# First batch's attention blocks turned with all 128 rows into one bank per head, and the first feed-forward weight converted in two halves

## The chip, the cores and the metric

The kernel runs on one core of a Trainium2 chip. The metric is device time in microseconds (us) of that core. The engines are TensorE (PE in the profile; PEld are its weight loads), VectorE (DVE), ScalarE (ACT), GpSimd (POOL) and SyncE (SP, which here only issues DMAs). Matrix products land in PSUM, which this kernel divides into eight banks; the other engines work in SBUF.

## What is computed

Three stages follow each other: attention with rotary positions (4 batches, 8 heads, 576 positions, 64 wide), a feed-forward block with shifted inputs, and a second one with a spatial gate.

```python
scores = scale * np.matmul(q_rot, k_rot.transpose(0, 1, 3, 2))
attn = np.exp(scores - np.max(scores, axis=-1, keepdims=True))
attn = attn / (np.sum(attn, axis=-1, keepdims=True) + 1e-09)
x = np.matmul(attn, v)                       # then heads side by side: (4, 576, 512)

xk = mu_k * x + (1.0 - mu_k) * x_prev        # x_prev: x one position earlier
xr = mu_r * x + (1.0 - mu_r) * x_prev
k = np.maximum(xk @ w_k, 0.0)                # w_k: 512 x 1024
x = sigmoid(xr @ w_r) * (k * k @ w_v)

h = np.maximum(x @ w_in, 0.0)
u, v = h[..., :512], h[..., 512:]            # v is normalised over its 512 entries
gated = u * (w_spatial @ v + b_spatial)
out = gated @ w_out
```

## The kernel before

**Units.** Attention works on pairs of heads (16 pairs: 4 a batch) and, within a pair, on blocks of 128 queries. 576 is four and a half blocks, so two pairs make nine *units*: eight of 128 queries of both heads of one pair, and a *tail* unit (every m with m % 9 == 4) that holds the 64 left over from each of the two pairs. The first batch is units 0 to 17. For unit m the kernel does this:

- scores (`scores`, L338): eight products with 64 rows each, into `s`, two tiles (one for each head) of two banks each. In the batches after the first, `q` and `k` are split in a high and a low part and L330 makes 12 products instead;
- maxima (`top`, L342, DVE), one for each head;
- exponentials (`expo`, L347, ACT), one for each head, into `pf`. The score products of unit m+1 reuse the banks of `s`, so those of head 0 need the first exponential of unit m and those of head 1 the second;
- sums and their reciprocals: `total` (ACT), `norm` (DVE), `spread` (ACT, writes `rb`);
- turns (`turn`, L367, PE): the 512 *main* keys of `pf` are transposed. Each head takes eight transposes of 64 rows, `turn(0)` and `turn(1)`. Both write a tile `t` of two banks: what comes from query rows 0 to 63 goes to the first bank, that from rows 64 to 127 to the second, so each bank holds a half of both heads. `turn(0)` stands before the scores of unit m+1 in PE's queue, `turn(1)` behind them;
- turn of the rest (`turn_rest`, L380 and L381, PE): the last 64 keys of both heads and `rb`, two transposes of 128 rows, into a tile `u` of one of the two banks of the pool `m`;
- copies out of PSUM into `pt`: `take(1)` and `take(0)` (L395, ACT), and `take_rest` (L402, DVE);
- for every second unit, and for the tail, the product with the values (`values`, L409, ten products over 128 rows, into the other pool `m` bank), and `gather` (L421, DVE) into `xt`.

**Between.** The rotary steps of later pairs (`prep`, L249 and L257) and the conversion of weights run on DVE, ACT and POOL beside the units. The weights arrive as 64-bit floats. Converting one piece of 512 columns (`weight64`) takes three DVE instructions (L156, L164, L165), two on ACT (L160, L171) and two on POOL (L168, L174). `w_k` has eight such pieces: two for each of its four row blocks; `wk_ready` lists them, and each product of the first feed-forward layer (`k_dot`, L505) waits for all eight. `w_v` has eight more.

**Feed-forward.** `feed(b, h)` is the first feed-forward block for half h of batch b. It needs all of batch b's units, so batch b's feed runs beside the units of batch b+1, and nothing of that kind can run beside the first batch.

**What sets the order.** Each action is a step of a `Plan`: an engine, an assumed duration, what it depends on, a rank, and which slot of a resource it takes or gives back (`take`, `give`; L205 gives `t` one slot, that is the tile of two banks as a whole). `order` (L62) plays the steps through and takes for each engine the ready step of lowest rank; the order that comes out is what each engine's queue holds. The waits on the chip are not the plan's: they are set afterwards from which tile an instruction writes and reads.

## Time and profile before

| | |
|---|---|
| time, three runs | 768.33, 773.10, 777.09 us (median 773.1) |
| profiled execution | 773.33 us, of which the span in the profile is 771.5 us |
| granted TensorE clock, mean | 0.989 |
| PE | 723.5 us busy, 94% of the span |
| DVE | 473.5 us, 61% |
| ACT | 456.4 us, 59% |
| POOL | 112.5 us, 15% |
| transposes of 64 rows, L367 | 1152 |
| the copies L395 of them | 144, mean 589 ns |

The times of rows below are us from the start of the span. In the 40 slices of the page, PE is at 3 to 8 tenths in the first six (to 116 us) and at 9 in nearly every later one. The granted clock is a share of full speed: 1.00 stands for 2.4 GHz and 0.50 for 1.2 GHz; a stretch between is a mixture of the two.

### The profile page before, as it was taken

What the parts mean: (1) busy time and instruction counts of PE and PEld (TensorE: products, weight loads), DVE (VectorE), ACT (ScalarE), POOL (GpSimd) and SP (SyncE); (2) the same over time, 40 slices, a digit from 0 to 9 for tenths busy, and PEclk for the clock granted to TensorE, in tenths of its full rate; (3) what the DMA queues carried; (4) which work ended last, traced back from release to release, by engine and by line L of the source; (5) the groups of instructions that cost most, each with busy time, mean ns of one, the idle gap of its engine ahead of it and who ended that gap; (6) DMA issues with size and microseconds to landing.
All of it is one profiled execution on the core that took longest, in us unless ns stands there. A gap on an engine that the chain in (4) does not pass through costs nothing.

```text
span 771.5 us, 15273 instructions
## 1 busy us (share of the span) xinstructions
PE 723.5 (94%) x6208; PEld 636.9 (83%) x6208; DVE 473.5 (61%) x881; ACT 456.4 (59%) x1045; POOL 112.5 (15%) x132
## 2 busy tenths in 40 slices
PE   3787779899999999999999999999999999999998
PEld 2554448698798788888798799989989999998997
DVE  5769898886886986886866444247363342545111
ACT  4667888887877887777887554246334332533211
POOL 2243245012002021022031000002020000101000
PEclk9989899999999999999999999999999999999999
DMA  8355432442543353443351085082201212010101
GB/s 296 117 158 167 132 116 79 149 122 87 177 132 135 119 173 107 134 143 105 119 174 63 16 297 192 25 264 83 62 1 63 63 47 78 17 31 1 62 1 62
DMA packets 35273, 84.20 MB, mean 109 GB/s; under 512 B 4545, under 2 KB 10433, under 8 KB 35202
## 3 DMA queue, kind: packets, MB, share of 16 engines
q1 hardware_dynamic: 34658, 82.63, 32.6%
q8 instruction: 49, 0.80, 0.4%
q10 hardware_dynamic: 544, 0.59, 0.3%
q14 instruction: 22, 0.18, 0.1%
HBM read 60.65 MB, written 22.55 MB: 108 GB/s over the span
## 4 chain that ended last, share of the span: by engine, by line
PE 87%; ACT 5%; DMA 4%; DVE 3%; issue 1%; SPq 1%; ACTq 0%; DVEq 0%
PE v L409 12%; PE mk L505 12%; PE mv L544 11%; PE sp L680 8%; PE r L680 7%; PE u L680 7%; PE hv L744 7%; PE o L680 7%; PE t L367 6%; PE s L330 5%; PE s L338 3%; ACT pt L395 3%; PE u L380 1%; PE s L327 1%; DMA I-6413_6414<-xd 1%; DMA wi<-wd 1%
## 5 line engine op out<-in xcount | busy, mean ns | idle before, releaser
L342 DVE TENSOR_REDUCE sm<-s 128x1 f32<-128x576 f32 x144 | 106.0, 750 | 28.4 <-PE s L330 20.3
L347 ACT ACTIVATE pf<-s,sm 128x576 f32<-128x576 f32 x144 | 106.6, 749 | 10.6 <-DVE sm L342 10.5
L505 PE MATMUL mk<-x,wk 128*128 128x288 f32 x768 | 110.8, 300 | 0.7 <-DVE pt L400 0.7
L544 PE MATMUL mv<-kh,wv 128*128 128x288 f32 x512 | 109.2, 299 | 0.9 <-DVE pt L402 0.5
L505 PEld LDWEIGHTS mk<-x,wk 128*128 128x128 f32 x768 | 104.0, 190 | 1.7 <-PE u L377 0.8
L395 ACT COPY pt<-t 128x512 f32<-128x512 f32 x144 | 77.6, 589 | 41.5 <-PE t L367 40.7
L409 PE MATMUL v<-pt,vt 128*64 128x256 f32 (+1 forms) x640 | 90.8, 433 | 8.5 <-ACT pt L395 8.2
L367 PEld LDWEIGHTS t<-ident,pf 64*128 64x128 f32 x1152 | 56.3, 141 | 47.0 <-ACT pf L347 22.6
L367 PE MATMUL t<-ident,pf 64*128 64x64 f32 x1152 | 68.8, 232 | 21.0 <-ACT pf L347 20.9
L544 PEld LDWEIGHTS mv<-kh,wv 128*128 128x128 f32 x512 | 83.8, 188 | 2.7 <-issue 1.2
L409 PEld LDWEIGHTS v<-pt,vt 128*64 128x64 f32 x640 | 45.7, 144 | 42.9 <-ACT pt L395 11.3
L544 PE MATMUL mv<-kl,wv 128*128 128x288 f32 x256 | 75.7, 296 | 0.4 <-DVE kl L523 0.4
L680 PE MATMUL sp<-ws,vn 128*128 128x288 f32 x384 | 53.9, 295 | 0.0
L680 PE MATMUL r<-xr,wr 128*128 128x288 f32 x384 | 52.5, 296 | 1.2 <-ACT vs L550 1.2
L680 PE MATMUL o<-g,wo 128*128 128x288 f32 x384 | 52.9, 296 | 0.5 <-ACT os L803 0.5
L680 PEld LDWEIGHTS r<-xr,wr 128*128 128x128 f32 x384 | 51.7, 188 | 1.8 <-ACT vs L550 1.5
L680 PEld LDWEIGHTS sp<-ws,vn 128*128 128x128 f32 x384 | 52.4, 188 | 0.7
L680 PEld LDWEIGHTS o<-g,wo 128*128 128x128 f32 x384 | 51.7, 188 | 1.4 <-ACT os L803 1.2
L680 PE MATMUL u<-x,wi 128*128 128x288 f32 x384 | 52.0, 296 | 0.0
L680 PEld LDWEIGHTS u<-x,wi 128*128 128x128 f32 x384 | 51.6, 188 | 0.3
L249 DVE TENSOR_TENSOR raw<-raw,cst 128x1152 f32<-128x1152 f32 (+1 forms) x34 | 46.7, 1380 | 5.8 <-DMA raw<-kp 5.3
L544 PEld LDWEIGHTS mv<-kl,wv 128*128 128x128 f32 x256 | 48.2, 188 | 0.6 <-DVE kl L523 0.6
(346 smaller groups left out, 1182.0 us busy)
## 6 DMA issues: line engine op xcount, KB each, us to landing
raw<-kp SPq DMA_DIRECT2D x15, 576.0 KB, 3.9
raw<-qp SPq DMA_DIRECT2D x15, 576.0 KB, 4.7
vt<-vp SPq DMA_DIRECT2D x16, 320.0 KB, 3.8
xd<-xt SPq DMA_DIRECT2D x16, 288.5 KB, 4.3
vd<-vs SPq DMA_DIRECT2D x32, 144.0 KB, 1.8
v<-vd SPq DMA_DIRECT2D x16, 288.0 KB, 2.8
out<-os SPq DMA_DIRECT2D x15, 288.0 KB, 2.1
wi<-wd SPq DMA_DIRECT2D x8, 512.0 KB, 9.1
```

What stands on the lines that cost most here:

```text
L249: nc.vector.tensor_tensor(t["raw", k][:, :, z], t["raw", k][:, :, z], cst[:, :, z], op=ALU.mult)
L330: nc.tensor.matmul(ps[j][:, h, :HALF], t[a, 0][r, 128 * c:128 * c + 128], t[b, 1][r, x], **f)
L338: nc.tensor.matmul(o, q[r, 128 * c:min(128 * c + 128, S)], k[r, h * HALF:(h + 1) * HALF], start=True, stop=True)
L342: nc.vector.tensor_reduce(st["sm"][:, 0, j:j + 1], st["s"][j][:, :, :HALF], axis=AX.XY, op=ALU.max, negate=True)
L347: nc.scalar.activation(st["p"][:, j, :].rearrange("p (a b) -> p a b", a=2), st["s"][j][:, :, :HALF], AF.Exp, bias=st["sm"][:, 0, j:j + 1], ...
L367: nc.tensor.transpose(st["t"][:, h, 4 * n + c, :], st["p"][r, n, k:k + 128], ident[r, r])
L395: nc.scalar.copy(o, st["t"][:, :, 4 * k:4 * k + 4, :])
L409: nc.tensor.matmul(pv[HEAD[j], z], v[:, 4 * j + c if c < 4 else 8 + j, :], pt[:, 4 * j + c if c < 4 else 8, z], start=c == 0, stop=c == 4)
L505: nc.tensor.matmul(ps[:, :HALF], wk[w][:, c, fc * 128:(fc + 1) * 128], a[:, c, :], start=k == 0, stop=k == 11)
L544: nc.tensor.matmul(xs["v", dc][:, :HALF], wv[w][:, fc, dc * 128:(dc + 1) * 128], a, start=k == 0, stop=k == 23)
L680: nc.tensor.matmul(ps[:, h, :HALF], w, a[:, h * HALF:(h + 1) * HALF], start=m == 0, stop=m == n - 1)
L744: nc.tensor.matmul(ps[:, :FS], x[a][:, d, c:c + 128], wi[w][:, d, FS:], start=k == 0, stop=k == 11)
```

## The change

Two edits, and a third that follows from them.

1. *Turns of the first batch.* One tile `both` of the two banks is made once. In units 0 to 17 each head's main keys are turned by four transposes of 128 rows (`turn_whole`) into one bank; the rest goes into a bank of `both` too, and no longer into one of `m`. The plan sees two slots, `t`, and gives one to each of the three turns of a unit; each copy gives its slot back. Head 0 and head 1 are copied by `take_whole` (ACT, 512 columns from one bank), the rest by `take_rest` as before. In tail units the transposes keep 64 rows (eight a head); their copies become four of 256 columns.
2. *`w_k` in two parts.* The pieces 0, 2, 4, 6 (columns 0 to 511) stand first, with the old ranks; the pieces 1, 3, 5, 7 get ranks 16.5 to 19.5, among `w_v`'s ranks of 17 to 21.9. Products for the first four column blocks wait for the first four pieces alone, the others for the second four.
3. Units from 18 on turn as before; the plan now calls their tile's slot `d`, and it waits for all copies of the first batch.

```diff
@@ -124,6 +124,8 @@
     v_dram = [dram.tile([128, 4, S], F32, tag=f"vd{b}", name=f"vd{b}") for b in range(B)]
 
     cst = at.tile([128, 2, S], F32, name="cst")
+    both_banks = ps_t.tile([128, 2, 8, 64], F32, tag="t", name="both")
+    whole = []
     ends = [[at.tile([128, 128], F32R, tag=f"qe{i}{k}", name=f"qe{i}{k}") for k in range(2)] for i in range(2)]
     ident = const.tile([128, 128], F32, name="ident")
     mix4 = const.tile([128, NP, 4], F32, name="mix4")
@@ -202,7 +204,7 @@
     wv = [wpool.tile([128, NFC, DM], F32R, tag=f"wB{i}", name=f"wv{i}") for i in range(2)]
 
     second, fed = {}, set()
-    plan = Plan({"m": 2, "e": 4, "t": 1, "ww": WB, "wg": GB})
+    plan = Plan({"m": 2, "e": 4, "t": 2, "d": 1, "ww": WB, "wg": GB})
     add = plan.add
 
     def which(m):
@@ -368,8 +370,8 @@
 
         def turn_rest(slot):
 
-            pt, p = ps_m.tile([128, 4, 128], F32, tag=f"m{slot}", name=f"u{m}"), st["p"]
-            st["u"] = pt
+            p = st["p"]
+            pt = st["u"] = ps_m.tile([128, 4, 128], F32, tag=f"m{slot}", name=f"u{m}") if isinstance(slot, int) else slot
             if tail:
                 for u in range(2):
                     for k in range(2):
@@ -379,6 +381,31 @@
             else:
                 nc.tensor.transpose(pt[:, 0, :], p.rearrange("p a b -> p (a b)")[:, 512:640], ident)
                 nc.tensor.transpose(pt[:, 1, :], st["r"].rearrange("p a b -> p (a b)"), ident)
+
+        def turn_whole(n, slot):
+
+            pt = st["t", n] = both_banks[:, slot].rearrange("p a b -> p (a b)").rearrange("p (c q) -> p c q", c=4)
+            p = st["p"]
+            if tail and n < 2:
+                for u in range(2):
+                    for c in range(4):
+                        k = 64 * n + 128 * c
+                        nc.tensor.transpose(pt.rearrange("p c (h q) -> p (c h) q", h=2)[:, 4 * u + c, :],
+                                            p[HEAD[n], u, k:k + 128], ident[HEAD[n], HEAD[n]])
+            elif n < 2:
+                for c in range(4):
+                    k = 64 * n + 128 * c
+                    nc.tensor.transpose(pt[:, c, :], p[:, n, k:k + 128], ident)
+            else:
+                turn_rest(pt)
+
+        def take_whole(n):
+            x = st["t", n].rearrange("p c (h q) -> p (c h) q", h=2)
+            for u in range(len(into)):
+                if tail:
+                    nc.scalar.copy(turned_to(u)[:, 4 * n:4 * n + 4, 256:320], x[:, 4 * u:4 * u + 4, :])
+                else:
+                    nc.scalar.copy(turned_to(u)[:, 4 * n:4 * n + 4, 128 * part:128 * part + 128], st["t", n])
 
         def turned_to(u):
             d = into[u if tail else 0]
@@ -436,14 +463,28 @@
         nm = add("DVE", 0.17, norm, [t], m - 0.3)
         sp = add("ACT", 0.26, spread, [nm], m - 0.3)
         late = [y for d in into for y in freed.get(d["n"] - PTB, [])]
-        t = add("PE", 0.27, lambda slot: turn(0), [exps[m, 0]], m + -0.02, take="t", kind="s")
-        turned[m, 0] = x = add("PE", 0.27, lambda: turn(1), [exps[m, 1], t], m + 0.05, kind="s")
-        x = add("ACT", 0.59, lambda: take(1), [x] + late, m - 0.2, 0.05)
-        x = add("ACT", 0.59, lambda: take(0), [x] + late, m - 0.2, give=t)
-        turned[m, 1] = t = add("PE", 0.55 if tail else 0.22, turn_rest, [sp], m + 0.2, take="m", kind="t")
-        y = add("DVE", 0.55 if tail else 0.42, take_rest, [t] + late, m - 0.2, give=t)
-        for d in into:
-            d["ev"] += [x, y]
+        if w[0][0] < EXACT:
+            ready = [[exps[m, 0], exps[m, 1]] if tail else [exps[m, 0]], [exps[m, 1]], [sp]]
+            xs = []
+            for n in range(3):
+                turned[m, n] = t = add("PE", (0.5, 0.5, 0.8)[n] if tail else (0.44, 0.44, 0.22)[n], lambda slot, n=n: turn_whole(n, slot),
+                                       ready[n], m + 0.1 * n, take="t", kind="t")
+                if n < 2:
+                    xs.append(add("ACT", 0.68 if tail else 0.59, lambda n=n: take_whole(n), [t] + late, m - 0.2, give=t))
+                else:
+                    xs.append(add("DVE", 0.55 if tail else 0.42, take_rest, [t] + late, m - 0.2, give=t))
+            whole.extend(xs)
+            for d in into:
+                d["ev"] += xs
+        else:
+            t = add("PE", 0.27, lambda slot: turn(0), [exps[m, 0]] + whole, m + -0.02, take="d", kind="s")
+            turned[m, 0] = x = add("PE", 0.27, lambda: turn(1), [exps[m, 1], t], m + 0.05, kind="s")
+            x = add("ACT", 0.59, lambda: take(1), [x] + late, m - 0.2, 0.05)
+            x = add("ACT", 0.59, lambda: take(0), [x] + late, m - 0.2, give=t)
+            turned[m, 1] = t = add("PE", 0.55 if tail else 0.22, turn_rest, [sp], m + 0.2, take="m", kind="t")
+            y = add("DVE", 0.55 if tail else 0.42, take_rest, [t] + late, m - 0.2, give=t)
+            for d in into:
+                d["ev"] += [x, y]
         if part and k != 3 or tail:
             v = add("PE", 2.9 if duo["cols"] > 256 else 2.3, values, duo["ev"] + [vloads[w[0][0]]], m + 0.9, take="m", kind="v")
             i = w[0][0]
@@ -523,7 +564,7 @@
                 nc.vector.tensor_tensor(kl, xs["r", q], raw(kh), op=ALU.subtract)
 
             q = fc // 2
-            z = p = add("PE", 1.58, lambda slot, k_dot=k_dot: k_dot(0, slot), done + wk_ready + [second.get("close")], rank(fc), take=room)
+            z = p = add("PE", 1.58, lambda slot, k_dot=k_dot: k_dot(0, slot), done + wk_ready[fc // 4] + [second.get("close")], rank(fc), take=room)
             free = kept.get(("kl", 8 * b + 4 * h + q - RLB))
             r = add("ACT", 0.42, relu, [p, free], rank(fc) - 2, give=z)
             last.append(p)
@@ -567,7 +608,7 @@
         if i < ROT // 2:
             prep(i)
     mix_ready = add("DVE", 0.4, mixes, [add("SP", 1.0, load_mixes, [], 0, 12)], 6)
-    wk_ready, wv_ready = [], []
+    wk_ready, wv_ready = ([], []), []
 
     def weight_steps(t, r, old=()):
         w = a = add("SP", 0.4, lambda slot: t[0](slot), old, r - 8 if not old else r, 8 if not old else 5, take="ww")
@@ -579,10 +620,11 @@
         a = add("POOL", 1.4, lambda: t[6](), [a], r, give=g)
         return a if len(t) == 7 else add("SP", 0.4, lambda: t[7](), [a], r, 3.5, give=w)
 
-    for c in range(16):
+    for c in (0, 2, 4, 6, 1, 3, 5, 7, *range(8, 16)):
         k = c < 8
         args = (w_k, c // 2, wk[0][:, c // 2], wk[1][:, c // 2], c % 2) if k else (w_v, c - 8, wv[0][:, c - 8], wv[1][:, c - 8], 0)
-        (wk_ready if k else wv_ready).append(weight_steps(weight64(*args), 1.8 * c if k else 17 + 0.7 * (c - 8)))
+        (wk_ready[c % 2] if k else wv_ready).append(
+            weight_steps(weight64(*args), 17 + 0.7 * (c - 8) if not k else 16 + c / 2 if c % 2 else 1.8 * c))
     early = ([(w_r, c, 0, w_dram[0][:, c]) for c in range(NP)]
              + [(w_in, c, q, w_dram[1 + q][:, c]) for q in (1, 0) for c in range(NP)]
              + [(w_out, c, 0, w_dram[3][:, c]) for c in range(NP)])
```

How the queues change, in three places. `pf7` and `pf8` are the exponentials of units 7 and 8, `rb7` the spread reciprocals, `s16` to `s19` the scores of units 8 and 9; in brackets stand the engines whose semaphore the instruction waits for.

PE, from the scores of unit 8 to the first turn of unit 8. Before:

```order
L338 MATMUL s16_600<-rot1_1_276,rot1_0_279 128x288
L338 MATMUL s17_601<-rot1_1_276,rot1_0_279 128x288
L367 MATMUL t7_588<-ident_95,pf7_562 128x64 x8
L380 MATMUL u7_621<-ident_95,pf7_562 128x128 [waits PE_49]
L381 MATMUL u7_621<-ident_95,rb7_585 128x128 [waits Activation_49]
L367 MATMUL t8_634<-ident_95,pf8_630 128x64 [waits PE_49,Activation_49]
L367 MATMUL t8_634<-ident_95,pf8_630 128x64 x7
```

And of the change:

```order
L340 MATMUL s16_525<-rot1_1_254,rot1_0_257 128x288
L340 MATMUL s17_526<-rot1_1_254,rot1_0_257 128x288
L398 MATMUL both_91<-ident_96,pf7_507 128x128 [waits Activation_49]
L398 MATMUL both_91<-ident_96,pf7_507 128x128 x3
L382 MATMUL both_91<-ident_96,pf7_507 128x128
L383 MATMUL both_91<-ident_96,rb7_533 128x128
L398 MATMUL both_91<-ident_96,pf8_551 128x128 [waits DVE_49,Activation_49]
L398 MATMUL both_91<-ident_96,pf8_551 128x128 x3
```

The sequence is the same; the turns are four of 128 rows. New are two waits: the turn of head 1 of unit 7 waits for ACT (the value it waits for is the one that head 0's copy reaches), and the first turn of unit 8 waits for DVE (the copy of unit 7's rest).

ACT, in the same unit. Before:

```order
L358 COPY rb7_585<-sm7_534 128x128 [waits DVE_49]
L160 ACTIVATE I-459_460<-I-459_460 128x512 [waits DMAHW4_49]
L171 CAST wk0_99<-I-575_576 128x512 [waits Pool_49]
L395 COPY pt3_624<-t7_588 128x2x4x64 [waits PE_49]
L395 COPY pt3_624<-t7_588 128x2x4x64
L347 ACTIVATE pf8_630,sm8_602<-s16_600,sm8_602 128x576 [waits DVE_49]
```

And of the change:

```order
L360 COPY rb7_533<-sm7_475 128x128 [waits DVE_49]
L408 COPY pt3_535<-both_91 128x4x128 [waits PE_49]
L173 CAST wk0_100<-I-509_510 128x512 [waits Pool_49]
L408 COPY pt3_535<-both_91 128x4x128 [waits PE_49]
L349 ACTIVATE pf8_551,sm8_527<-s16_525,sm8_527 128x576 [waits DVE_49]
```

One of the two copies has moved ahead. The second one still stands in front of the next unit's exponential, and the value of PE's semaphore that it waits for is reached only by L383, the last transpose of the unit's rest.

DVE, in the same unit. Before:

```order
L354 RECIPROCAL sm7_534<-sm7_534 128x2 [waits Activation_49]
L421 TENSOR_TENSOR xt1_597<-v6_564,pt2_424 128x320 [waits PE_49]
L342 TENSOR_REDUCE sm8_602<-s16_600 128x1 [waits PE_49]
L402 COPY pt3_624<-u7_621 128x2x128 [waits PE_49]
L342 TENSOR_REDUCE sm8_602<-s17_601 128x1
```

And of the change:

```order
L448 TENSOR_TENSOR xt1_521<-v6_495,pt2_376 128x320 [waits PE_49]
L356 RECIPROCAL sm7_475<-sm7_475 128x2 [waits Activation_49]
L344 TENSOR_REDUCE sm8_527<-s16_525 128x1 [waits PE_49]
L429 COPY pt3_535<-both_91 128x2x128 [waits Activation_49]
L344 TENSOR_REDUCE sm8_527<-s17_526 128x1
```

The copy of the rest stands between the two maxima of the next unit in both. Before it waits for PE; in the change it waits for ACT, for the second of the copies above. It stands like this in 13 of the units 1 to 17, in front of both maxima in units 7 and 10, behind both in the other two.

## Rows read from the trace of the kernel before

**Rows 1.** The page's chain of work that ended last, shares of the span by engine.
```profile
PE 87%; ACT 5%; DMA 4%; DVE 3%; issue 1%; SPq 1%; ACTq 0%; DVEq 0%
```

**Rows 2.** Busy time by stretch: start:end, length, engines (instructions), granted clock, DMA share, GB/s.
```profile
36.00:46.00 10.00, 9.22 (x70) 5.58 (x72) 7.00 (x13) 6.56 (x18) 5.51 (x3) 0.66 0.46 148
...
46.00:84.00 38.00, 26.90 (x276) 17.54 (x275) 32.98 (x61) 30.52 (x74) 12.14 (x11) 1.00 0.46 139
...
84.00:93.00 9.00, 8.88 (x70) 5.06 (x66) 7.92 (x17) 6.51 (x18) 3.18 (x2) 0.62 0.53 186
...
120.00:220.00 100.00, 96.74 (x996) 82.56 (x994) 81.41 (x155) 80.90 (x204) 18.68 (x16) 1.00 0.34 113
220.00:600.00 380.00, 373.37 (x3305) 335.93 (x3302) 237.78 (x447) 239.97 (x557) 44.68 (x55) 1.00 0.37 122
```

**Rows 3.** Timeline, units 8 to 9: start, length, engine, line, operation, count, idle before.
```profile
55.63 1.19 PE L338 MATMUL s<-rot,rot 64*128 64x288 f32 x8
...
56.66 0.41 PE L367 MATMUL t<-ident,pf 64*128 64x64 f32 x8
56.86 0.76 DVE L342 TENSOR_REDUCE sm<-s 128x1 f32<-128x576 f32 x1 [0.91 <-PE s L338]
...
57.00 0.33 PE L380 MATMUL u<-ident,pf 128*128 128x128 f32 x1
...
57.11 1.07 ACT L395 COPY pt<-t 128x512 f32<-128x512 f32 x2 [0.52 <-PE t L367]
...
57.16 0.27 PE L381 MATMUL u<-ident,rb 128*128 128x128 f32 x1
57.53 0.41 DVE L402 COPY pt<-u 128x256 f32<-128x256 f32 x1
57.86 0.75 DVE L342 TENSOR_REDUCE sm<-s 128x1 f32<-128x576 f32 x1
58.07 0.76 ACT L347 ACTIVATE pf<-s,sm 128x576 f32<-128x576 f32 x1
58.79 0.75 ACT L347 ACTIVATE pf<-s,sm 128x576 f32<-128x576 f32 x1
...
60.52 0.40 PE L338 MATMUL s<-rot,rot 64*128 64x288 f32 x1
```

**Rows 4.** Timeline, the scores of units 10, 11 and 12, and a value product between.
```profile
65.18 1.19 PE L338 MATMUL s<-rot,rot 64*128 64x288 f32 x8
...
70.58 0.40 PE L338 MATMUL s<-rot,rot 64*128 64x288 f32 x1
...
72.39 2.38 PE L409 MATMUL v<-pt,vt 128*64 128x256 f32 x20 [0.80 <-ACT pt L395]
...
74.70 0.47 PE L367 MATMUL t<-ident,pf 64*128 64x64 f32 x8
...
75.00 1.19 PE L338 MATMUL s<-rot,rot 64*128 64x288 f32 x8
```

**Rows 5.** Timeline, DVE's three instructions that convert one piece of a weight.
```profile
65.34 0.42 DVE L156 TENSOR_SCALAR I-718_719<-I-459_460 128x512 f32<-128x512 f32 x1
...
65.79 0.43 DVE L164 TENSOR_SCALAR I-459_460<-I-459_460 128x512 int32<-128x512 int32 x1
...
66.25 0.69 DVE L165 SCALAR_TENSOR_TENSOR I-718_719<-I-718_719,I-459_460 128x512 int32<-128x512 int32 x1
```

**Rows 6.** Timeline, three value products of 320 columns, and the first two feed-forward products.
```profile
40.97 4.59 PE L409 MATMUL v<-pt,vt 128*64 128x320 f32 x20
...
52.49 2.91 PE L409 MATMUL v<-pt,vt 128*64 128x320 f32 x20 [0.74 <-ACT pt L395]
...
87.50 5.21 PE L409 MATMUL v<-pt,vt 128*64 128x320 f32 x20
...
115.98 3.18 PE L505 MATMUL mk<-x,wk 128*128 128x288 f32 x12
...
120.70 1.83 PE L505 MATMUL mk<-x,wk 128*128 128x288 f32 x12
```

## The prediction

> **What bounds the kernel now.** I read the page's chain of the work that ended last first: PE holds 87% of the span in it, and no other engine more than 5% [rows 1]. Then the busy time by stretch. From 120 us on PE is full: 96.74 us of 100, then 373.37 of 380 [rows 2]. Work there comes in PE's own order, so what delays the start of the second batch delays the end one for one. Between 46 and 84 us, in the first batch, PE is busy for 26.90 us of 38 and DVE for 32.98 [rows 2]: nothing is full, and a chain of waits sets the pace. So the question is how long that chain becomes in units 0 to 17.
>
> Its links stand in the timeline. I call T the end of a unit's scores. For unit 8, T = 55.63 + 1.19 = 56.82, and the next scores end at 60.52 + 0.40 = 60.92: 4.10 us later. In between: the second turn ends at 57.07, the rest's at 57.43; the two copies hold ACT until 58.18 (57.11 + 1.07); DVE takes the first maxima, the copy of the rest (57.53 to 57.94), the second maxima (to 58.61); the exponentials start at 58.07 and 58.79, and the second ends at 59.54; the scores of head 1, which need it, end 1.38 later [rows 3]. Where a value product stands between, the distance is longer: unit 11's scores end at 70.98 and unit 12's at 76.19, 5.21 apart, with the product of 2.38 us beginning at T + 1.41 and ending just before the turn at 74.70 [rows 4].
>
> **The turns and their waits.** The tile `both` is one tile, and the waits that are set for it treat it as one. The three order places show the result: the turn of head 1 waits for the copy of head 0; the copy of head 1 waits for the last transpose of the rest, although it reads the other bank; the copy of the rest waits on ACT for the copy of head 1; and the next unit's first turn waits for the copy of the rest. What was three loose copies is now one line, and the copy of the rest stands in front of the second maxima. I follow it from T, in a transition without a value product.
>
> - Turns. Eight transposes of 64 columns take 0.41, so about 0.05 each; with 128 columns I take 0.10 each, an estimate from that row; the last counts with the 0.33 of a single one [rows 3]. Four: 0.33 + 3 x 0.10 = 0.63. The rest's first transpose begins 0.07 before the turn of before ended (57.00 against 57.07), so PE is free for head 1 at T - 0.07; its turn ends at T + 0.56, and the two of the rest 0.20 later, at T + 0.76. Head 0's copy, which head 1's turn waits for, is done by then: it needs only the first exponential, a scores' length earlier.
> - Head 1's copy starts 0.04 behind its releaser, as 57.11 does behind 57.07: T + 0.80. It takes 0.59 (the table's mean) and ends at T + 1.39. In before both were over at T + 1.36.
> - Copy of the rest: 0.10 behind (57.43 to 57.53), then 0.41: T + 1.49 to T + 1.90. In before T + 0.71 to T + 1.12.
> - Second maxima: begin 0.08 before that copy's end, as in 57.86 against 57.94: T + 1.82, and with 0.75 end at T + 2.57. In before T + 1.79.
> - Exponentials: the first stands behind head 1's copy on ACT, and starts at about T + 1.3 (before T + 1.25), so it ends near T + 2.1 and isn't the limit. The second starts 0.10 behind the maxima, T + 2.67, and ends at T + 3.42 (before T + 2.72).
> - Scores end 1.38 later: T + 4.80 against T + 4.10. That is **+0.70**.
>
> The next unit's first turn waits for the copy of the rest (T + 1.90) as well as for the exponential (T + 2.1): nothing. Behind head 1's copy on ACT wait only the first exponential, as said, and conversion work, which isn't on the path.
>
> There are 18 transitions, from unit 0 to unit 18. Nine are like this: 9 x 0.70 = 6.3. In unit 10 the copy of the rest stands in front of both maxima (unit 7, where it does too, has a value product before it): it ends at T + 1.90, the maxima end at T + 2.57 and 3.23, the second exponential runs from T + 3.33 to 4.08, and the scores end at T + 5.46. The same place was at 70.98 - 66.37 = 4.61 in before [rows 4]: +0.85. Seven have a value product. It waits for head 1's copy, T + 1.44 instead of T + 1.41, +0.03; the copy of the rest only feeds its last products, later. Behind it the turn takes 0.63, and the scores can start 0.56 behind its start instead of 0.30 (74.70 to 75.00): +0.26. 7 x 0.29 = 2.0. In the two tail units the first turn now waits for both exponentials and stands in front of the scores. If it binds, the scores end 0.56 + 1.19 = 1.75 behind the second exponential instead of 1.38; if the value product of that place covers it, nothing. I take 0.2 each, half, 0.4 in all (bounds 0 and 0.74). The first transition, before the pattern has settled, I give 0.3 (bounds 0 and 0.7). Sum: 6.3 + 0.85 + 2.0 + 0.4 + 0.3 = 9.85, about **10 us**.
>
> Weighed against a rule: the rows of before show two engines at work in different banks at once, ACT copying from `t` from 57.11 on while PE turns the rest into `u` at 57.16 [rows 3]. The Trainium skill, PSUM — Partial Sum Buffer, section "PSUM bank collisions raise a hardware error", says that two engines on different banks run clean, and that the dependency is one of bank, not of more. By that rule no wait between the two banks is needed and the sum would be the 776 of the rival "banks apart" below, by the waits that are set 783; no run of before shows a wait of this tile.
>
> **The weight.** The program order has 12 conversions of pieces in front of the maxima of unit 18 before, and 11 after: one piece leaves the first batch. Per piece DVE spends 0.42 + 0.43 + 0.69 = 1.54 us [rows 5]. Its load, one DMA on SP's queue, moves with it; the DMA engines are at 0.46 to 0.53 in the first batch [rows 2] and have room. At most 1.5 us is gained, if all of it stood on the path; but DVE's idle time is where it lies (32.98 of 38 busy, and the chain above leaves DVE free from the second maxima to the next first ones). I take 0. The conversions pushed behind unit 18 meet a DVE at 81.41 of 100 and an ACT at 80.90, with PE full [rows 2]: hidden, 0. There remains the feed-forward's first product: it now needs four pieces only, but stands behind the second turn of unit 19 in PE's queue, later by one unit's scores. In the rows it ran at 115.98 for 3.18 us, the next one at 120.70 for 1.83 [rows 6]. If the move lets it run at the higher clock, 1.35 is gained; if PE stands idle in its stead, up to 1.83 is lost. I take 0.
>
> The profiled execution took 773.33 us, practically the median of 773.1. 773.33 + 9.85 = 783.2: forecast **783 us**. Its own range: 783.2 - 1.35 - 1.5 - 0.7 (no cost in tails and first) = 779.6, and with the dearer ends 783.2 + 1.83 + 0.34 + 0.4 = 785.8; the 0.10 of a transpose could be 0.16 (the pitch from 57.00 to 57.16 [rows 3]), which adds 5 x 0.06 = 0.3 in ten transitions, 3 us: up to 788.8. So 779 to 789.
>
> **The rivals.**
>
> *A clock that falls more often.* The granted clock is 0.66 in 36 to 46 us and 0.62 in 84 to 93, at 1.00 in 46 to 84 [rows 2]; both low stretches are those of the tail units, where value products are far apart and PE only turns and scores. A value product of 320 columns costs 4.59 and 5.21 us there against 2.91 at full clock: 1.68 and 2.30 more [rows 6]. Longer waits stretch every gap between value products. If two to five more places fall, at about 2.0 each, 4 to 10 us come on top: 787 to 793, say 788. Against it: the stretches between are not at the edge in any row, 46 to 84 is at 1.00 throughout. The Trainium skill, TensorE: Matmul & The Clock Gate, section "Part 4: PE-mode transpose", says that transposes do not count as PE-busy for the clock in the same way as products do. That would let the clock fall in gaps that only turns fill, as here, and the trace agrees so far as its low stretches are such (0.66, 0.62).
>
> *A clock that stays up.* Full-row turns keep PE's rows busier; if this saves both low stretches and the first feed-forward product, 1.68 + 2.30 + 1.35 = 5.3 are gained from the sum: 778. Against it: the transposes' columns are the same in total per head, and the waits grow.
>
> *Banks apart.* If the waits between the banks are met before they bind (the rest's transposes being early, or the copies shorter), the copy of the rest stays where it was and only the longer turn is left: 0.11 in each of the ten without a value product, 0.29 in seven, 1.1 + 2.0, with nothing in the tails: 776. Against it: the rest stands behind head 1's turn in PE's queue, so its copy can't be early.
>
> *Not slower.* One of the two copies leaves ACT's place in front of the exponential. If DVE placed the copy of the rest behind both maxima on the chip's path, the first exponential would start at about T + 0.85 and the second right behind it, some 0.35 earlier than now in ten transitions: -3.5; with 2.0 for the value transitions and -1.5 for the piece of weight, 773.3 - 3.0 = 770. It decides if the copy of the rest ends before T + 1.04, the end of the first maxima less the lag. The order of DVE, where it stands between the maxima, speaks against it.
>
> **How the numbers follow.** My forecast gets 0.55, the falling clock 0.18, the clock that stays up 0.12, banks apart 0.08, not slower 0.07. The range 774 to 792 leaves out the last and the far end of the second, less than 2 in 10. One per cent, about what a measurement of this kernel can tell from no change, is 765.4 to 780.8. Slower by over 1%: nearly all of the forecast's 0.55 less its low end (0.10), and the falling clock's 0.18, 0.63, less something for costs that overlap otherwise than drawn: 0.58. Within 1%: the low end, 0.12, 0.08 and most of 0.07: 0.37. Faster: 0.05, where the clock that stays up and the mechanism of the last rival meet.
>
> **What would show it.** In the timeline of the changed kernel: a copy of the rest that begins 1.5 us after T instead of 0.7, its idle time ended by ACT; second maxima at T + 1.8; scores 4.8 apart without a value product; `both` released by ACT at head 1's turn with no idle time. The second batch should begin about 10 us later, and the time behind it stay the same. I am wrong if the scores stay 4.1 apart, if the first batch's clock differs, or if PE's time behind 120 us changes by more than 2 us.

## The result and the profile after

The changed kernel takes **783.76 us** (median of 4 runs, 780.26 to 785.18); the kernel before, beside it, 771.89 (4 runs, 768.33 to 777.09). The ratio is 1.0136, with a 95% interval of 1.0097 to 1.0176: slower, by about 12 us. The forecast was 783, the range 774 to 792. The profiled execution has a span of 781.6 us against 771.5 and a mean granted clock of 0.987 against 0.989.

The chain of work that ended last, shares of the span by engine:

```profile
PE 85%; ACT 5%; DVE 4%; DMA 3%; issue 1%; SPq 0%; POOL 0%; ACTq 0%; DVEq 0%
```

PE still sets the end, with a little less than the 87% of [rows 1], and DVE has one share more. The changed transition stands in the timeline from unit 8 to unit 9, the same place as [rows 3]; the columns are as there.

```profile
58.33 1.24 PE L340 MATMUL s<-rot,rot 64*128 64x288 f32 x8
...
59.50 0.66 PE L398 MATMUL both<-ident,pf 128*128 128x128 f32 x4
59.60 0.76 DVE L344 TENSOR_REDUCE sm<-s 128x1 f32<-128x576 f32 x1 [1.15 <-PE s L340]
...
60.10 0.27 PE L383 MATMUL both<-ident,rb 128*128 128x128 f32 x1
60.41 0.59 ACT L408 COPY pt<-both 128x512 f32<-128x512 f32 x1 [0.35 <-PE both L383]
60.89 0.75 ACT L349 ACTIVATE pf<-s,sm 128x576 f32<-128x576 f32 x1
61.03 0.42 DVE L429 COPY pt<-both 128x256 f32<-128x256 f32 x1 [0.67 <-ACT pt L408]
61.37 0.75 DVE L344 TENSOR_REDUCE sm<-s 128x1 f32<-128x576 f32 x1
...
62.15 0.74 ACT L349 ACTIVATE pf<-s,sm 128x576 f32<-128x576 f32 x1 [0.42 <-DVE sm L344]
62.37 1.90 PE L340 MATMUL s<-rot,rot 64*128 64x288 f32 x8
```

T is 58.33 + 1.24 = 59.57. The new line of waits can be read from the brackets: head 1's copy (60.41) was released by L383, the last transpose of the rest; DVE's copy of the rest (61.03) by that copy on ACT, after 0.67 us in which DVE stood idle; the second maxima follow it (61.37), and the second exponential them (62.15). The scores end at 62.37 + 1.90 = 64.27, 4.70 after T, where [rows 3] had 4.10.

In unit 10 the copy of the rest stands in front of both maxima. T is 69.88 there:

```profile
70.72 0.59 ACT L408 COPY pt<-both 128x512 f32<-128x512 f32 x1 [0.58 <-PE both L383]
...
71.34 0.42 DVE L429 COPY pt<-both 128x256 f32<-128x256 f32 x1 [0.63 <-ACT pt L408]
...
71.68 1.41 DVE L344 TENSOR_REDUCE sm<-s 128x1 f32<-128x576 f32 x2
...
73.20 0.73 ACT L349 ACTIVATE pf<-s,sm 128x576 f32<-128x576 f32 x1
...
73.94 1.37 PE L340 MATMUL s<-rot,rot 64*128 64x288 f32 x8
```

They end at 75.31, T + 5.43; in [rows 4] it was 4.61.

How far the kernel after lies behind the one before, by the end of a unit's scores (us):

| unit | before | after | behind |
|---|---|---|---|
| 4 | 34.03 | 34.53 | 0.50 |
| 9 | 60.92 | 64.27 | 3.35 |
| 12 | 76.19 | 80.91 | 4.72 |
| 14 | 85.91 | 92.06 | 6.15 |
| 15 | 94.14 | 98.77 | 4.63 |
| 18 (first of the second batch) | 107.93 | 115.97 | 8.04 |
| 21 | 126.07 | 134.18 | 8.11 |
| end of span | 771.5 | 781.6 | 10.1 |

8 us are lost in the first batch and 2 more later. Between units 14 and 15 something is won back. That is the clock, by the same stretches as [rows 2]:

```profile
36.00:46.00 10.00, 8.46 (x66) 5.87 (x66) 7.47 (x16) 6.39 (x18) 2.65 (x3) 0.83 0.49 172
46.00:84.00 38.00, 30.66 (x189) 19.22 (x190) 29.08 (x53) 27.04 (x64) 9.74 (x10) 0.96 0.33 108
84.00:93.00 9.00, 6.55 (x46) 4.63 (x42) 5.88 (x13) 6.91 (x20) 3.80 (x3) 0.81 0.57 175
```

The granted clock is 0.83 and 0.81 in the two stretches of the tail units, where it was 0.66 and 0.62, and 0.96 in the one between, where it was 1.00. The value products of 320 columns show both sides:

```profile
41.98 3.45 PE L436 MATMUL v<-pt,vt 128*64 128x320 f32 x20
...
53.92 3.89 PE L436 MATMUL v<-pt,vt 128*64 128x320 f32 x20
...
94.11 2.91 PE L436 MATMUL v<-pt,vt 128*64 128x320 f32 x20
```

The two at the tails took 4.59 and 5.21 before [rows 6] and take 3.45 and 2.91 now; the one at 53.92 took 2.91 and takes 3.89.

The start differs too, and the granted clock doesn't tell it: it is given as 1.00 for the first 30 us of the kernel before. A value product of 256 columns takes 4.53 us there, against 2.38 in [rows 4]. The changed kernel's turn of one head takes 0.66 us at 18.54 already, as at 59.50. The first line is the kernel before, the second the changed kernel:

```profile
22.86 4.53 PE L409 MATMUL v<-pt,vt 128*64 128x256 f32 x20 [0.55 <-ACT pt L395]
```

```profile
18.54 0.66 PE L398 MATMUL both<-ident,pf 128*128 128x128 f32 x4 [1.41 <-ACT pf L349]
```

So the changed kernel leaves its slow start earlier in these two profiles: from unit 1 to 2 it takes 5.37 us, the kernel before 5.84.

### The profile page after: what moved, and what is told of

Read it like the earlier page. It is cut to its first block, busy times and chain, and to the rows that moved or that the text cites. A ratio compares the mean times of both kernels' runs of the same rounds, so it can differ in the third digit from the quotient of the medians.

```text
span 781.6 us, 15025 instructions
## 1 busy us (share of the span) xinstructions
PE 734.1 (94%) x6080; PEld 641.8 (82%) x6080; DVE 475.3 (61%) x881; ACT 459.1 (59%) x1049; POOL 109.4 (14%) x132
## 4 chain that ended last, share of the span: by engine, by line
PE 85%; ACT 5%; DVE 4%; DMA 3%; issue 1%; SPq 0%; POOL 0%; ACTq 0%; DVEq 0%
PE mv L585 11%; PE mk L546 11%; PE v L436 10%; PE sp L722 8%; PE r L722 7%; PE u L722 7%; PE hv L786 6%; PE o L722 6%; PE s L332 5%; PE t L369 4%; PE s L340 3%; PE both L398 2%; PE s L329 1%; PE u L382 1%; ACT pf L349 1%
## 5 line engine op out<-in xcount | busy, mean ns | idle before, releaser
L422 ACT COPY pt<-t 128x512 f32<-128x512 f32 x108 | 58.5, 589 | 29.7 <-PE t L369 29.3
L369 PEld LDWEIGHTS t<-ident,pf 64*128 64x128 f32 x864 | 39.1, 138 | 18.7 <-issue 6.9
L369 PE MATMUL t<-ident,pf 64*128 64x64 f32 x864 | 48.1, 229 | 2.6 <-ACT pf L349 2.6
```

The source lines that it names most:

```text
L369: nc.tensor.transpose(st["t"][:, h, 4 * n + c, :], st["p"][r, n, k:k + 128], ident[r, r])
L422: nc.scalar.copy(o, st["t"][:, :, 4 * k:4 * k + 4, :])
```

## Reading runs at one clock

The runs of one and the same kernel differ by their mean granted clock. Beside the experiments the kernel before was run 63 times: at 0.993 its runs average 769.7 us (14 runs), at 0.984 773.0 (19), at 0.980 775.4 (8). A straight line through the 63 falls by 0.435 us for each 0.001. In the table below the last column moves each run to 0.993 by that slope and takes the mean. It is a fit, good to about 1 us: what a lower clock costs depends on what runs in the stretch, and the mean leaves out the slow start.

| kernel | median us (runs) | ratio, 95% interval | median clock | at clock 0.993 |
|---|---|---|---|---|
| before | 772.7 (63) | | 0.984 | 769.9 |
| after | 783.76 (4) | 1.0136 [1.0097, 1.0176] | 0.986 | 780.1 |
| turns only | 783.99 (4) | 1.0127 [1.0066, 1.0188] | 0.984 | 779.9 |
| weight only | 766.36 (10) | 0.9924 [0.9892, 0.9955] | 0.993 | 766.3 |
| after, two tiles | 771.07 (10) | 0.9980 [0.9953, 1.0007] | 0.991 | 770.3 |
| after, rest in `m` | 771.61 (10) | 0.9989 [0.9962, 1.0017] | 0.991 | 771.0 |
| after, rest copied late | 778.66 (10) | 1.0074 [1.0044, 1.0103] | 0.989 | 776.8 |
| after, first product put back | 782.55 (4) | 1.0136 [1.0091, 1.0181] | 0.983 | 778.0 |
| weight only, six products unread | 777.31 (10) | 1.0057 [1.0028, 1.0085] | 0.998 | 779.4 |
| after, six products unread | 792.80 (4) | 1.0269 [1.0220, 1.0318] | 0.989 | 791.1 |
| weight only, two products unread | 768.23 (10) | 0.9934 [0.9914, 0.9954] | 0.994 | 768.5 |
| weight only, later pieces held | 785.66 (4) | 1.0171 [1.0115, 1.0228] | 0.985 | 782.3 |
| before, rest copied late | 772.24 (10) | 0.9987 [0.9966, 1.0008] | 0.994 | 772.3 |

At one clock the change costs 780.1 - 769.9 = 10.2 us.

## The experiments

The theory: the tile `both`, waited for as one, puts three copies in one line, and that line costs most of the loss. The rivals: the longer turns, the clock, or the weight edit.

### Turns only

```diff
-    wk_ready, wv_ready = ([], []), []
+    wk_ready, wv_ready = [], []
...
-    for c in (0, 2, 4, 6, 1, 3, 5, 7, *range(8, 16)):
+    for c in range(16):
```

> The changed kernel with the old order of the weight pieces (all eight pieces of w_k at their old ranks, every product of the first feed-forward layer waits for all eight). In the program the first feed-forward product then stands again ahead of unit 20's scores. Theory (the line of waits in the first batch costs about 8 us, and 1.9 us of the 10 come from the first feed-forward product that moved behind unit 20's scores): the first batch stays as long as in the changed kernel, and the end comes 1.9 us earlier than there, near 782 us, a ratio of 1.010 to 1.013 to the kernel before. Rival (the weight edit itself is what costs, by conversions pushed into the second batch): most of the loss goes, 773 to 777, ratio under 1.007.

783.99 us, ratio 1.0127. The rival falls: without the weight edit the loss is all there (779.9 at one clock, after 780.1). The 1.9 us that the theory wanted back don't show there. In the profiles the time from the end of unit 18's scores to the end is 664.47 us, 1.2 less than in the changed kernel (665.63, below). The stretch from 146.15 to 166.15 us has a granted clock of 0.91, with PE busy for 16.82 us of 20: something was given back there, in a program whose second batch is laid out differently. This run doesn't settle the size of that term.

### Weight only

The kernel before, with the opposite of that edit.

> The kernel before with the weight edit alone: two parts of w_k, the turns as before. The first feed-forward product keeps its old place in PE's queue. Theory (one piece less in the first batch is worth nothing, and the later pieces are hidden): the time of before within 1.5 us, ratio 0.998 to 1.002. Rival 1 (the piece stood on the path): 1.5 us gained or more, ratio 0.998 or lower. Rival 2 (conversions in the second batch delay it): 775 to 780, ratio 1.004 to 1.010.

766.36 us, ratio 0.9924: rival 1, in sign, but four times its size, 6.2 us. The stretches of [rows 2] and [rows 6] show where most of it is:

```profile
36.00:46.00 10.00, 8.05 (x92) 5.24 (x94) 7.99 (x18) 8.28 (x21) 5.04 (x4) 1.00 0.74 241
...
84.00:93.00 9.00, 6.67 (x70) 4.28 (x68) 8.31 (x15) 8.19 (x21) 3.08 (x2) 1.00 0.57 187
```

The clock stays at 1.00 in both stretches of the tail units. Both value products of 320 columns there take 2.91 us, the transitions that hold them 5.81 and 5.74 instead of 8.16 and 8.23. Of the 6.8 us that unit 18's scores come earlier, 4.8 are in these two transitions. (At one clock the whole gain is 3.6.) Two transitions at full clock are 0.5 shorter each (from unit 3 to 4: 4.69 instead of 5.21; from unit 10 to 11: 4.10 instead of 4.61). In the second of these the copy of the rest now stands between the maxima instead of in front. Behind unit 21's scores the kernel needs 645.34 us, before 645.43: what was put into the second batch is hidden there. Why the clock holds at the tails with this order of work no run shows; the last experiment shows it holding at one of them without this edit.

### Two tiles

```diff
-    both_banks = ps_t.tile([128, 2, 8, 64], F32, tag="t", name="both")
+    pw = ps_w.enter_context(tc.tile_pool(name="ps_w", bufs=1, space=PSUM, side="right"))
+    banks2 = [pw.tile([128, 8, 64], F32, tag=f"w{i}", name=f"both{i}") for i in range(2)]
...
-            pt = st["t", n] = both_banks[:, slot]...
+            pt = st["t", n] = banks2[slot]...
```

(The pool is closed before unit 18's turn, which takes its two banks as one tile again.)

> The changed kernel with the two banks as two tiles, in the same order of instructions on every engine; only the waits differ: head 1's copy waits for its own four transposes, the copy of the rest for the rest's two. Theory (the waits across the banks are the price): in a transition without a value product head 1's copy starts at T + 0.63 instead of T + 0.84, the copy of the rest at T + 0.90 instead of T + 1.46, the second maxima at T + 1.24 instead of T + 1.80, and the scores end 4.2 apart instead of 4.7; ten of these give 4.8 us, those with a value product up to 1.4: 777 to 780 us, ratio 1.006 to 1.009, the rest being the moved feed-forward product and longer turns. Rival (the longer turns and the clock are the price, not the waits): within 1.5 us of the changed kernel, ratio 1.012 to 1.015.

771.07 us, ratio 0.998: 12.7 us less than the changed kernel, of which 9.8 at one clock. That is well below the 777 to 780 of the theory, which had 6.2 us of gain. The order of instructions is the same on every engine. The same transition, from unit 8, with T = 51.17:

```profile
51.10 0.66 PE L402 MATMUL both<-ident,pf 128*128 128x128 f32 x4
...
51.71 0.27 PE L387 MATMUL both<-ident,rb 128*128 128x128 f32 x1
51.80 0.59 ACT L412 COPY pt<-both 128x512 f32<-128x512 f32 x1 [0.31 <-PE both L402]
52.08 0.42 DVE L433 COPY pt<-both 128x256 f32<-128x256 f32 x1
52.28 0.75 ACT L350 ACTIVATE pf<-s,sm 128x576 f32<-128x576 f32 x1
52.43 0.75 DVE L345 TENSOR_REDUCE sm<-s 128x1 f32<-128x576 f32 x1
...
53.21 0.74 ACT L350 ACTIVATE pf<-s,sm 128x576 f32<-128x576 f32 x1
53.76 1.57 PE L341 MATMUL s<-rot,rot 64*128 64x288 f32 x8
```

Head 1's copy begins at T + 0.63, released by its own turn (L402); the copy of the rest at T + 0.91, beside it; the second maxima at T + 1.26; the scores end at T + 4.16. The numbers expected were 0.63, 0.90, 1.24 and 4.2.

So the line is as long as the theory says, and yet more comes back than it counts. Unit 18's scores end at 102.67, 13.3 us earlier than in the changed kernel. Six transitions run at full clock in both profiles. Together they give 2.0 us: 0.54 (unit 8 to 9), 0.55 (17 to 18), and about 0.2 each in the two with a value product of 256 columns (9 to 10, 11 to 12) and the two that lead into a tail unit. Nearly all the rest lies in transitions in which one of the two kernels has a low clock. How much of the 9.8 is the line itself, and how much the clock that went with it, no run separates.

In these rows ACT (51.80 to 52.39) and DVE (52.08 to 52.50) copy from the two banks at once. This is the rule weighed in the prediction: the Trainium skill, PSUM — Partial Sum Buffer, section "PSUM bank collisions raise a hardware error", asks for a dependency within one bank only. The rows agree with it.

### The rest in `m` again

```diff
-                                       ready[n], m + 0.1 * n, take="t", kind="t")
+                                       ready[n], m + 0.1 * n, take="t" if n < 2 else "m", kind="t")
...
+            if n == 2:
+                return turn_rest(slot)
```

> The changed kernel with the turn of the rest written to a bank of the pool m again, as before the change; the main keys keep their four transposes of 128 rows and their bank per head, and the two banks stay one tile. The order of instructions is that of the changed kernel; head 1's copy waits for its own turn, the copy of the rest for the rest's transposes. Theory (the whole price of the waits comes from the rest having joined the tile): as with two tiles, 769 to 773 us, ratio 0.996 to 1.001. Rival (the two heads' banks hinder one another as well, so that only separate tiles help): 775 to 781, ratio 1.004 to 1.011.

771.61 us, in the theory's range, as with two tiles (771.0 against 770.3 at one clock). The tile of two banks may stay one tile: what cost the time is that the rest was turned into it.

### The rest copied late

```diff
-                    xs.append(add("DVE", ..., take_rest, [t] + late, m - 0.2, give=t))
+                    xs.append(add("DVE", ..., take_rest, [t] + late, m + 0.45, give=t))
```

> The changed kernel with one number altered: the copy of the rest ranks behind both maxima of the next unit on DVE (it stands there in all units now). All waits stay. Theory (it is the second maxima behind that copy that is late): second maxima at T + 0.8 to T + 1.55, the first exponential stays at T + 1.3, the second follows it at T + 2.05, scores 4.1 to 4.2 apart: 5 us back, 777 to 780, ratio 1.006 to 1.010. Rival (head 1's copy, late on ACT in front of the first exponential, is enough to cost it; or the next unit's first turn then waits for the later copy): no gain, ratio 1.012 to 1.015.

778.66 us, ratio 1.0074, in the theory's range; 3.3 us less at one clock, where 5 were expected. The transition from unit 8, T = 60.17:

```profile
60.55 1.41 DVE L344 TENSOR_REDUCE sm<-s 128x1 f32<-128x576 f32 x2
...
61.02 0.59 ACT L408 COPY pt<-both 128x512 f32<-128x512 f32 x1 [2.02 <-PE both L383]
61.50 0.75 ACT L349 ACTIVATE pf<-s,sm 128x576 f32<-128x576 f32 x1
61.88 0.41 DVE L429 COPY pt<-both 128x256 f32<-128x256 f32 x1
...
62.23 0.74 ACT L349 ACTIVATE pf<-s,sm 128x576 f32<-128x576 f32 x1
```

Head 1's copy is as late as in the changed kernel (T + 0.85), and still the scores end at T + 4.18, because both maxima are done before the copy of the rest. Four other transitions without a value product take 4.16 or 4.17. So in these it is the place in front of the second maxima that the loss goes through, as the theory has it; ACT's late copy alone costs 0.1. What became of the rest of the 5 us is shown in one place only: with the copy of the rest planned later, PE has unit 8's value product behind unit 9's first turn (it starts 2.8 us after T, not 0.7), and unit 10's scores end 6.34 after unit 9's, where it was 5.61. From unit 11 to 12, with a value product too, it is 5.61 in both. The profile's clock is lower as well (0.982 against 0.987).

### The first feed-forward product put back

```diff
+    first_k = []
...
-        scored[m] = s = add("PE", ..., need + [exps.get((m - 1, j)) for j in range(2)], m - 1.0, kind="s")
+        scored[m] = s = add("PE", ..., need + [exps.get((m - 1, j)) for j in range(2)] + ([first_k[0]] if m == 20 else []), m - 1.0, kind="s")
...
+            first_k.append(p)
```

> The changed kernel with one dependence more in the plan: unit 20's scores come behind the first feed-forward product, as in the kernel before; unit 19's second turn and rest come ahead of them too. Theory (the product that moved leaves twelve products more to do behind unit 21's scores, 1.9 us): the stretch from the end of unit 21's scores to the end is 645.4 us as in the kernel before, not 647.4; 781 to 783 us, ratio 1.010 to 1.014. Rival (TensorE only waits elsewhere for it): the same as the changed kernel, 783 to 785, ratio 1.013 to 1.017.

782.55 us: too near the changed kernel to tell by the medians alone; at one clock 778.0 against 780.1, 2.1 less. The trace tells it better. The stretch from the end of unit 21's scores to the end, in the kernel before, the changed kernel, and this one:

```profile
126.07:771.50 645.43, 631.43 (x5400) 575.42 (x5396) 372.72 (x695) 367.18 (x827) 67.52 (x86) 1.00 0.30 99
```

```profile
134.18:781.60 647.42, 634.48 (x5412) 577.72 (x5408) 375.87 (x699) 370.09 (x833) 71.47 (x88) 1.00 0.30 98
```

```profile
133.74:778.30 644.56, 631.78 (x5400) 575.28 (x5396) 374.22 (x698) 368.86 (x829) 68.50 (x87) 1.00 0.29 99
```

The changed kernel has 5412 products left at that point, the other two 5400: the twelve of one column block, 1.83 us in [rows 6]. They make 647.42 - 645.43 = 2.0 us in this stretch, and they go away with the dependence. But the stretch begins behind the place where the product moved, so what was done there instead isn't counted. From the end of unit 18's scores, ahead of that place, the same three kernels need:

```profile
107.93:771.50 663.57, 646.96 (x5553) 587.70 (x5548) 388.22 (x727) 382.71 (x866) 77.16 (x93) 1.00 0.30 100
```

```profile
115.97:781.60 665.63, 648.91 (x5551) 588.76 (x5550) 390.44 (x729) 383.31 (x867) 79.17 (x95) 1.00 0.31 101
```

```profile
113.95:778.30 664.35, 647.72 (x5551) 587.60 (x5550) 390.15 (x729) 383.62 (x867) 78.32 (x95) 1.00 0.30 101
```

The changed kernel needs 2.06 us more than the kernel before, and 1.28 of them go away with the product put back; in the kernel with the turns only it was 1.16. Where the other 0.8 lies no run shows.

### Later pieces held

The kernel with the weight edit alone, the pieces made in two further groups, each waiting for a unit's scores:

```diff
+        if m == 13:
+            pieces((1, 3, 5, 7), [scored[m]])
+        if m == 16:
+            pieces(range(8, 16), [scored[m]])
```

> The kernel before with the weight edit alone, and the second four pieces of w_k held until the scores of unit 13, those of w_v until the scores of unit 16: 7 conversions instead of 11 (and 12 in the kernel before) stand in front of the maxima of unit 18. Theory (a conversion costs the first batch only where it stands between two maxima or shifts the copy of the rest, not by its time): the first batch as long as with the weight edit alone, 764 to 768, ratio 0.989 to 0.995, unless the later products of the feed-forward have to wait. Rival (each piece costs the first batch 1.5 us and more): four pieces less give 4 to 6 us more, 760 to 762, ratio under 0.987.

785.66 us, far above both ranges. The first batch is no shorter with four conversions less: unit 18's scores end at 103.29 (weight only 101.16, with the low clock elsewhere). From the end of unit 7's scores to there both kernels run at full clock, this one first:

```profile
49.20:103.29 54.09, 40.02 (x416) 25.91 (x414) 39.67 (x80) 42.12 (x106) 6.32 (x5) 1.00 0.36 116
```

```profile
47.77:101.17 53.40, 40.57 (x415) 26.21 (x414) 46.36 (x94) 45.00 (x112) 17.13 (x16) 1.00 0.39 128
```

With 6.7 us less work on DVE the stretch is 0.7 us longer. So the time of the conversions taken out cost the first batch nothing, as I had put it. The second batch pays for the delay:

```profile
120.00:220.00 100.00, 87.87 (x824) 72.66 (x822) 86.93 (x150) 74.02 (x182) 30.91 (x23) 0.93 0.38 125
```

PE is busy for 87.87 us of 100 there, in [rows 2] for 96.74.

### Products that nobody reads

```diff
+            def filler(slot):
+                f = ps_m.tile([128, 512], F32, tag=f"m{slot}", name=f"f{m}")
+                for _ in range(6):
+                    nc.tensor.matmul(f[:, :HALF], qk[w[0][0]][0][:, 0:128], qk[w[0][0]][1][:, 0:HALF], start=True, stop=True)
```

> The kernel before with the weight edit alone, and in the first batch, behind the rest's transposes of each unit that no value product follows, six products of 128x128 by 288 columns into a free bank of m that nobody reads (they compute nothing that is used). TensorE waits there for about 1.3 us; the six take about 0.9. Theory (the clock falls where TensorE has had little to do, and each 0.001 of mean granted clock is worth about 0.5 us by the spread of the runs of one kernel): the stretches at 1.2 GHz in the first batch disappear, mean clock from 0.993 to 0.997 or more, 762 to 765 us, ratio 0.987 to 0.991. Rival (the clock does not follow that, or the products delay the next turn by as much): 766 to 770, ratio 0.992 to 0.997.

> The changed kernel with the same six unread products behind the rest's transposes of each first-batch unit that no value product follows. Theory (clock): mean clock from 0.986 to 0.995 or more, 4 to 5 us gained, 778 to 780 us, ratio 1.007 to 1.010; the 10 us that the waits cost stay, since the transitions at full clock stay 4.7 apart. Rival (the waits cost only through the clock): down to the time of before at the same clock, 768 to 771, ratio under 1.0.

777.31 and 792.80 us, above all the ranges that were expected. I had sized them wrongly. From the weight-only kernel with the six:

```profile
55.24 3.08 PE L451 MATMUL f<-rot,rot 128*128 128x288 f32 x12
```

Each product runs as two passes, and six take 3.08 us where 0.9 was assumed. A transition without a value product is 4.95 long there, not 4.10. They tell something of the clock. The changed kernel without and with them:

```profile
20.00:60.00 40.00, 32.91 (x209) 20.75 (x208) 28.87 (x53) 25.95 (x64) 10.89 (x10) 0.87 0.34 115
```

```profile
20.00:60.00 40.00, 38.24 (x259) 25.08 (x258) 29.18 (x53) 26.95 (x65) 11.33 (x11) 1.00 0.36 118
```

With PE busy for 38.24 us of 40 the clock stays at 1.00; with 32.91 it is 0.87 on the mean. But busy time alone doesn't tell it: in [rows 2] PE is busy for 26.90 us of 38 at 1.00. And the changed kernel with the six falls later, for longer than the one without them does anywhere:

```profile
80.00:93.00 13.00, 10.74 (x64) 7.47 (x60) 6.00 (x12) 6.04 (x15) 3.82 (x3) 0.99 0.29 82
93.00:103.00 10.00, 8.74 (x52) 5.70 (x54) 7.12 (x14) 6.84 (x20) 3.09 (x3) 0.50 0.40 126
```

Over the runs its median clock is 0.989, where 0.995 was expected and 0.986 is the changed kernel's. In the weight-only kernel the median clock of the runs rises from 0.993 to 0.998. The gain is far below the price. In the changed kernel the loss stays too: from unit 8 to 9, at full clock in both, it takes 5.34 us with the six, and the weight-only kernel with the six 4.94. So the rival that the waits cost only through the clock falls.

> As the kernel with the weight edit alone and six unread products behind the rest's transposes, but with two of them; one of the six took 0.51 us there, so that six filled 3.1 us where 1.3 are free. Two take 1.03. Theory (the clock follows what TensorE had to do, and nothing is lost where the products fit): mean clock 0.995 or more, against 0.993 with the weight edit alone; the transitions without a value product at 4.1; 763 to 766 us, ratio 0.988 to 0.992. Rival (two products are not enough to hold the clock): clock 0.993, 766 to 768, ratio 0.992 to 0.995.

Two products: 768.23 us, clock 0.994, the time of the kernel without them within its interval (0.9934 against 0.9924). By the clock and the ratio the rival holds: these two products didn't keep the clock up. In its profile it falls at about 24 to 27, 82 to 89 and 112 to 116 us.

### The kernel before with the rest copied late

The edit of "the rest copied late" in the kernel before.

> The kernel before with one number altered: the copy of the rest ranks behind both maxima of the next unit on DVE and stands there in all units; turns, tiles and weights as before. It stands in front of both maxima in units 10 and 13 before, between them in most. Theory (what the weight edit gains by itself, 3 us at one and the same clock, comes from how it lays DVE's work between the maxima, not from the piece of weight): 2 to 3 us less at the same clock, 767 to 771 us, ratio 0.993 to 0.998. Rival (it is the split of the weight): the time of before, ratio 0.998 to 1.002.

772.24 us, 0.9987: by the number the rival's range, but not for its reason. Unit 10's transition is 4.10, as with the weight edit (4.61 before), so that half microsecond is DVE's order. The clock changes with the order too. The value product of the second tail runs at full clock, as with the weight edit:

```profile
85.84 2.91 PE L409 MATMUL v<-pt,vt 128*64 128x320 f32 x20 [0.55 <-ACT pt L395]
```

The one of the first tail doesn't (4.66 us). Unit 18's scores end at 103.94, 4.0 us earlier than before, and over the runs the median clock is 0.994 against 0.984. But the plan laid out the second batch anew as well, and from there on the kernel needs 666.46 us instead of 663.57. So a clock that holds at a tail can come without the split of the weight. What else the weight edit gains at one clock (3.6 in all by the fit) is not placed.

## The prediction against the runs

**The line of waits: right.** Step by step, from T, as forecast and as measured in unit 8: turn 0.63 and 0.66 long; head 1's copy at 0.80 and 0.84; copy of the rest at 1.49 and 1.46; second maxima at 1.82 and 1.80; second exponential at 2.67 and 2.58; scores' end at 4.80 and 4.70. In unit 10: 5.46 and 5.43. With the two tiles the line is gone and 9.8 of the 10.2 us with it; so the waits, not the turns, are the loss, in part by the clock that goes with them.

**The count of the line: wrong in part.** Nine transitions were put at +0.70. Four of them run at full clock in both profiles. Two show it: unit 8 to 9 (+0.60) and 17 to 18 (+0.59). The two that lead into a tail unit don't: from unit 12 to 13 it took 4.69 and takes 4.96, from unit 3 to 4 it took 5.21 and takes 4.96. So the term of 6.3 was too large for them. That all nine together differ by 6.2 in the profiles is luck, since the other five have a low clock in one kernel or the other.

**The value transitions: right where they can be read.** +0.29 each was forecast; those of 256 columns were longer by 0.16 (unit 9 to 10) and 0.39 (unit 11 to 12). Those of 320 columns hold a low clock in the changed kernel (3.89 above), and can't be compared.

**The tails: a little too dear at full clock.** 0.70 of the line and 0.2 for the turn were forecast. The transition from unit 4 to 5 takes 4.25 at full clock (weight only) and 4.95 where the changed order runs without a fall (the first product put back): 0.70 in all. In the changed kernel's own profile it is 6.11 against 4.80, with the scores at 2.23 us instead of 1.19: the rest is clock.

**The clock: both rivals at once.** It fell at more places, as the first rival had it (at about 25, 52 and 103 us, where the kernel before has no fall; at 25 that one is still in its slow start), and it held better at the tails, as the second had it. Neither decided: 0.987 against 0.989 in the profiles, 0.986 against 0.984 over the runs. I had weighed them as alternatives, each with one sign; in the rows both happen, and the falls lie at other places. At unit 18 the kernel is 8.04 us behind, not 9.85. Of this difference 1.5 is there by unit 4, where the sum had 0.3 + 0.70 + 0.29 + 0.70 = 1.99 and the table has 0.50. Behind it the tails won back 1.14 and 2.30 on their two value products, and the new falls took some of that: 0.98 on the product at 53.92.

The prediction named three signs of being wrong. The first, scores that stay 4.1 apart, didn't come. The second did: the clock of the first batch differs. The third, more than 2 us behind 120 us, is at its edge: 2.06 us from unit 18 on, PE busy for 1.95 more.

**The first feed-forward product: wrong.** I gave its move nothing, between bounds of -1.35 and +1.83. From the end of unit 18's scores on, the changed kernel loses 2.06, and 1.28 of it goes away when the product is put back: towards the dear end. Its later run has not even the higher clock (3.15 us at 126.72, before 3.18 in [rows 6]). The step that failed is taking 0 between two ends, where a row spoke for one of them: from 120 us on PE is full [rows 2], so that work left over from an idle stretch has to be paid for there. That it costs its whole time of 1.83 is not shown.

**The weight: wrong by itself.** I took 0, with a bound of 1.5 us of gain. Alone, the edit gains 6.2, in the profile most of it by a clock that holds at the tails. Its time on DVE is worth nothing, as argued (the pieces held back), but I had not seen that moving a piece lays other work anew around it. Beside the new turns none of the gain shows: 780.1 with the edit and 779.9 without it, at one clock. That the total came out so near the forecast is in part luck: the 2.06 missed in the second batch stand against the 1.8 that the first batch lost less than the sum had.

**The last rival, not slower:** not so. The place of the copy of the rest spoke against it, and even with that copy behind both maxima the first exponential starts at T + 1.33, not T + 0.85, as head 1's copy still stands in front of it; that kernel stays 6.9 us slower than before at one clock.

The fastest kernel here is the one with the weight edit and the old turns, 0.9924 of the kernel before. The full-row turns brought nothing once their waits were gone: with two tiles or with the rest in `m` the kernel stays 4 to 5 us behind it at one clock, of which the moved product is 1 to 2.

## What to carry to other kernels

When two users are put into one tile to save a buffer, follow each instruction that reads it to what it will wait for: here a copy of 0.42 us made the way to the next unit 0.6 us longer at full clock, because it waited for another engine's copy of another bank while the longest chain stood behind it in its own queue. A plan that counts slots doesn't show such a wait; the list of waits does. And an edit that shifts one step in a greedy plan should be read to the place where the order is equal again, since work that leaves an idle stretch has to be paid for in a full one.

## What the hardware showed

- One kernel's runs spread over 767.88 to 777.66 us, and most of that goes with the mean granted clock: 0.435 us for each 0.001, over 63 runs. A difference of 5 us between two single runs says nothing without their clocks.
- In the profile of the kernel before, the eight score products of the first units took 2.49 us and later ones 1.19, though the granted clock is given as 1.00 from 8 us on: the mean of a run leaves out what the clock costs at the start. How long that lasts differs: a value product at 22.86 still took 4.53 us there, while the changed kernel turned in 0.66 us at 18.54.
- A fall in the first batch lasted about 6.8 us at the tails before (0.50 from 37.6 to 44.4 and from 85.4 to 92.2) and 3.4 us in the changed kernel, at five places (from 24.5, 38.1, 51.8, 89.3 and 103.0). In the changed kernel with six unread products behind the turns it stayed at 1.00 from 20 to 60 us, and was at 0.50 from 93 to 103. The Trainium skill, TensorE: Matmul & The Clock Gate, section "Part 4: PE-mode transpose", says that transposes don't count as busy for the clock in the same way. These rows don't decide it: stretches of turns fell, and with products among the turns one stretch held and a later one did not. No run here replaced turns alone.
